# Infini-attention and GEGLU layers on one core: the first segment by halves, a plan that waits for loads, another prologue, and planner ranks that change with planned time

## The chip, the cores and the metric

The kernel runs on one core of a Trainium2 chip. The core has five engines that run side by side, each through its own list of instructions in order: TensorE (PE: matmuls, with their weight loads shown as PEld), VectorE (DVE), ScalarE (ACT), GpSimd (POOL) and SyncE (SP, which here issues the transfers). The metric is the device time of one execution in microseconds. A trace is of one profiled execution; its span runs from the first to the last instruction.

## The reference

Four steps follow each other on x of 2048 tokens by 512 features, all in bfloat16: attention, feed-forward, attention, feed-forward, each with a layer norm ahead and a residual sum behind; both attentions have the same weights, and both feed-forwards too.

```python
def _A_ref(x, wq, wk, wv, wo, beta):          # H = 32 heads of 16, N = 4 segments of L = 512
    ...
    for s in range(N):
        logits = jnp.einsum('bhqd,bhkd->bhqk', qs, ks) * scale + mask      # causal, inside the segment
        p = _softmax(logits, axis=-1)
        a_dot = jnp.einsum('bhqk,bhkd->bhqd', p, vs)
        pq = phi(qs)                                                        # t + 1 above 0, exp(t) below
        num = jnp.einsum('bhld,bhde->bhle', pq, M)
        den = jnp.einsum('bhld,bhd->bhl', pq, z)[..., None] + 1e-06
        a_mem = num / den
        o = g * a_mem + (1.0 - g) * a_dot
        outs.append(o)
        pk = phi(ks)
        M = M + jnp.einsum('bhld,bhle->bhde', pk, vs)
        z = z + jnp.einsum('bhld->bhd', pk)
    ...
def _B_ref(x, w_gate, w_up, w_down):          # hidden width 1792
    return _gelu(x @ w_gate) * (x @ w_up) @ w_down

x = x + _A_ref(_layernorm(x, axis=-1), A_wq, A_wk, A_wv, A_wo, A_beta)
x = x + _B_ref(_layernorm(x, axis=-1), B_w_gate, B_w_up, B_w_down)
x = x + _A_ref(...)
x = x + _B_ref(...)
```

A segment of an attention needs the memory M, z of the segments before it, and nothing else of them. The feed-forward works on each token by itself.

## The kernel before, in words

The work is cut into eight segments k = 0 to 7: 0 to 3 are the first attention and its feed-forward, 4 to 7 the second. Each has 512 tokens, four tiles of 128. All of x and all weights lie in SBUF. One tile `big` of PSUM holds eight banks of 512 floats.

A segment's attention: layer norm of the four tiles (statistics L544 and L553, scales on POOL L561 and L567, the normed rows L580), a transposition to `xnT` (a DMA transposition on SP, L477, or for some segments and for the feed-forward's norm in part by PE), then q, k and v by `product` (L516 to L521), which issues a matmul as four column tiles of 32. The results go from PSUM to SBUF by DVE or by ACT, whichever the plan gives them to (`evict`, L503 to L514). The scores run in steps (`steps_of`, L98): a step fills four banks with key rows times queries (L1274), one exp on ACT takes all four banks, 2048 columns, to a tile `pt` (L1344), and POOL zeroes what lies above the diagonal (L1317). A flush (L984) multiplies `pt` by the values in one bank; the values carry a column that sums the row, and DVE turns the bank (L1009), takes the reciprocal (L1013), scales (L1017) and turns back to `aT` (L1024). From the second segment on, `phi_q`, `phi_k`, `mem` and `upd` read and update the memory, and L1028 adds its part to `aT`.

The feed-forward of a segment starts with the out-projection `wo`, added to x (L1082), then a norm of its own, 14 gate tiles (gelu on ACT, from PSUM or, for the first `RAW` of them, from a copy in blocks), 14 up tiles multiplied in by DVE (L1169) and four down tiles, added to x. Segment 7, the last, is in `SPLIT`: its queries and its tokens go by halves of 256, so that the out-projection of a half needs only the four chunks of that half, and gate and up take two feature tiles of 256 columns in one bank.

The order on every engine is written out by a planner that runs while the program is built. `Clocks` and `Engine` hold a planned time for each engine; `items` are the pieces of PE work, sorted by a rank (`due`, from the tables `DUE`, `DUE_STEP` and `BIAS`, in units of a segment). The loop (L1468) takes a score step if its inputs are planned to be there and four banks are free, and else the first item in rank that is ready; if none is, it issues a filler, a product on the constant tile `warm` (L1495). Posted jobs of DVE, ACT, POOL and SP are taken by planned readiness plus a slack (`URGENT`, `PHI_SLACK` and others). PE and the other engines then run their lists in that order on the chip and wait where an input is not there.

Loads of the later x and of the weights are posted to SP with a planned time each (`X2`, `X3`, `WO`, `WG`, `WU`, `WD`, L381 to L393, L1417). The statistics of segment 2 are planned from 22.0 on (L1424) and those of segment 3 as soon as segment 1 has its keys and values (L1428); neither asks whether the rows have landed, and neither do the users of the weights.

The prologue is written by hand (L1348 to L1415): 19 warming matmuls (L417), POOL's masks and clearings (L460 to L462), the statistics of the first four tiles, scales for two tiles at a time (L1363), the first transpositions by PE (L619), and the first products of k and q; then planned time is set to 9.9 and the planner takes over.

## Time and profile before

| what | value |
|---|---|
| median of 3 runs | 563.38 us (562.55 to 564.78) |
| profiled execution | 565.31 us |
| its span | 563.6 us |
| mean granted clock of TensorE | 0.988 |
| PE busy | 543.1 us, 96% |
| DVE busy | 433.8 us, 77% |
| ACT busy | 406.1 us, 72% |
| POOL busy | 233.5 us, 41% |
| moved by DMA | 30.31 MB |

A group's row reads: line, engine, operation, output from input, shapes, count, then busy microseconds and mean nanoseconds of one, then the idle time of that engine just before these instructions and what ended it. A stretch's row reads: its start and end and length, the busy time of PE, PEld, DVE, ACT and POOL with their counts of instructions, the granted clock as a share, the busy share of the DMA engines and what they moved in GB/s. A row of the timeline reads: start, duration, engine, line, operation, output from input, shapes, count, and in brackets the idle time before and its releaser. SPq is SP's queue of transfers. Busy time of PE holds the fillers on `warm` too.

### The profile page before, as it was taken

How to read it: one execution, taken by the hardware profiler on the slowest of the kernel's cores; microseconds unless marked ns; L12 is line 12 of the kernel's file. 1: busy time of each engine (PE TensorE's matmuls, PEld its weight loads, DVE VectorE, ACT ScalarE, POOL GpSimd, SP SyncE). 2: the span in 40 equal slices, each digit the busy share in tenths (PEclk: the TensorE clock that was granted, in tenths of full speed). 3: DMA queues.
4: the chain of work that ended last, by engine and by line, in shares of the span. 5: the costliest groups of instructions: out<-in, count | busy, mean ns of one | idle time of the engine just before them, and what ended most of it. 6: DMA issues, size and time to landing. Idle time of an engine off the chain costs nothing.

```text
span 563.6 us, 28786 instructions
## 1 busy us (share of the span) xinstructions
PE 543.1 (96%) x13189; PEld 280.7 (50%) x13189; DVE 433.8 (77%) x829; ACT 406.1 (72%) x353; POOL 233.5 (41%) x403
## 2 busy tenths in 40 slices
PE   7994898999999999999999999999999999999997
PEld 3442354454454444555444444544445454555983
DVE  5985689878997887958997689979958796495361
ACT  4884789997989778938888487897879846951500
POOL 5432924554456344812467034734476333120000
PEclk9997799999999999999999999999999999999999
DMA  8298663003220102412134024241214003010001
GB/s 260 53 214 189 148 84 52 13 11 61 44 38 14 22 13 31 78 22 50 30 42 61 2 41 59 55 55 31 41 50 70 3 13 69 11 32 31 13 5 40
DMA packets 69626, 30.31 MB, mean 54 GB/s; under 512 B 54976, under 2 KB 69056, under 8 KB 69504
## 3 DMA queue, kind: packets, MB, share of 16 engines
q1 hardware_dynamic: 69360, 28.46, 26.5%
q8 instruction: 103, 1.69, 1.3%
q14 instruction: 19, 0.16, 0.1%
q10 hardware_dynamic: 144, 0.01, 0.0%
HBM read 9.71 MB, written 2.10 MB: 21 GB/s over the span
## 4 chain that ended last, share of the span: by engine, by line
PE 86%; DVE 7%; issue 2%; DMA 2%; ACT 1%; POOL 1%; SPq 1%; ACTq 0%; DVEq 0%; POOLq 0%
PE big L521 72%; PE big L1274 8%; PE big L984 6%; DVE x_sb L1082 1%; DVE st L544 1%; DMA x_sb<-in_A_x_dram 1%; ACT pt L1344 1%; DMA amT<-am 1%; DVE e L815 1%; DVE byq L1009 1%; SPq L365 1%; DVE xn L580 0%; DVE gel L512 0%; POOL vS L462 0%; POOL kB L461 0%
## 5 line engine op out<-in xcount | busy, mean ns | idle before, releaser
L1344 ACT ACTIVATE pt<-big 128x2048 bf16<-128x2048 f32 (+1 forms) x145 | 270.5, 1868 | 78.8 <-PE big L1274 72.2
L1317 POOL TENSOR_SCALAR_AFFINE_SELECT pt<-pt 64x256 bf16<-64x256 bf16 (+2 forms) x296 | 146.9, 521 | 256.7 <-ACT pt L1344 227.9
L521 PE MATMUL big<-xnT,wu_sb 128*32 128x512 bf16 (+1 forms) x2016 | 105.8, 356 | 0.9 <-DVE gel L1169 0.5
L521 PE MATMUL big<-wd_sb,gel 128*32 128x512 bf16 x1792 | 105.6, 380 | 0.4 <-DVE x_sb L1082 0.4
L521 PE MATMUL big<-xnT,wg_sb 128*32 128x512 bf16 (+1 forms) x2016 | 105.7, 356 | 0.2 <-issue 0.2
L1169 DVE TENSOR_TENSOR gel<-gel,big 128x512 bf16<-128x512 bf16 x112 | 75.1, 684 | 36.1 <-PE big L521 35.2
L521 PEld LDWEIGHTS <-wu_sb 128*32 128x32 bf16 x2016 | 52.1, 97 | 40.9 <-issue 5.6
L521 PEld LDWEIGHTS <-wg_sb 128*32 128x32 bf16 x2016 | 51.6, 97 | 40.0 <-issue 4.9
L521 PEld LDWEIGHTS <-gel 128*32 128x32 bf16 x1792 | 45.3, 97 | 43.9 <-issue 4.3
L1082 DVE TENSOR_TENSOR x_sb<-x_sb,big 128x512 bf16<-128x512 bf16 x64 | 42.8, 676 | 27.9 <-PE big L521 27.8
L1134 ACT ACTIVATE gel<-big 128x512 bf16<-128x512 f32 x70 | 38.5, 607 | 30.7 <-PE big L521 30.6
L1009 DVE STREAM_TRANSPOSE byq<-big 128x512 f32<-128x512 f32 x64 | 45.1, 704 | 16.3 <-PE big L984 9.1
L544 DVE BATCH_NORM_STATS2 st<-x_sb 128x6 f32<-128x512 bf16 x60 | 40.5, 675 | 6.4 <-DMA x_sb<-in_A_x_dram 6.1
L984 PE MATMUL big<-pt,vaug 128*32 128x192 bf16 (+4 forms) x1096 | 44.3, 266 | 0.2 <-DVE x_sb L1082 0.2
L521 PE MATMUL big<-xnT,wq_sb 128*32 128x512 bf16 (+1 forms) x528 | 36.0, 381 | 1.9 <-ACT pt L1344 1.2
L521 PE MATMUL big<-xnT,wk_sb 128*32 128x512 bf16 (+2 forms) x528 | 35.2, 380 | 0.7 <-DVE x_sb L1082 0.7
L521 PE MATMUL big<-wo_sb,aT 128*32 128x512 bf16 x512 | 32.1, 380 | 0.0
L683 POOL TENSOR_SCALAR kS<-kf,maskB 128x256 bf16<-128x256 bf16 x28 | 31.6, 1127 | 0.4
L521 PE MATMUL big<-wv_sb,xnT 128*32 128x512 bf16 x512 | 31.6, 380 | 0.0
L683 POOL TENSOR_SCALAR kS<-kf,maskA 128x256 bf16<-128x256 bf16 x28 | 29.6, 1057 | 1.6
L1274 PE MATMUL big<-q,kB 32*128 32x64 bf16 (+4 forms) x548 | 26.9, 269 | 3.3 <-ACT pt L1344 3.3
L580 DVE TENSOR_SCALAR xn<-x_sb,mv,rs 128x512 bf16<-128x512 bf16 x64 | 27.4, 477 | 3.4 <-POOL rs L567 2.7
(98 smaller groups left out, 628.0 us busy)
## 6 DMA issues: line engine op xcount, KB each, us to landing
vS<-vaug SPq DMA_DIRECT2D x16, 136.0 KB, 2.8
out_dram<-x_sb SPq DMA_DIRECT2D x16, 128.0 KB, 1.7
wg_sb<-in_B_w_gate_dram SPq DMA_DIRECT2D x8, 224.0 KB, 4.4
wd_sb<-in_B_w_down_dram SPq DMA_DIRECT2D x7, 256.0 KB, 4.7
kB<-kf SPq DMA_DIRECT2D x28, 64.0 KB, 2.9
wu_sb<-in_B_w_up_dram SPq DMA_DIRECT2D x8, 224.0 KB, 3.6
x_sb<-in_A_x_dram SPq DMA_DIRECT2D x3, 512.0 KB, 5.9
xnT<-xn SPq DMA_TRANSPOSE x48, 3.2
```

Of the source, the lines that this page charges most:

```text
L521: nc.tensor.matmul(out[r], lhsT=lhsT[:, r], rhs=rhs, start=start, stop=stop, tile_position=(0, 32 * c))
L544: nc.vector.bn_stats(out=self.st6[:, 0, :], in_=x_sb[:, self.tt0 + j, :])
L580: eng.tensor_scalar(out=xn[:], in0=x_sb[:, self.tt0 + j, :], scalar1=self.mv[:, j, 0:1], scalar2=self.rs[:, j, :], op0=ALU.subtract, op1=A ...
L683: eng.tensor_scalar(out=kS[:, b, :, :, u], in0=self.kf[:, b, :].rearrange("p (t h c) -> p t h c", h=2, c=Q)[:, :, 0, :], scalar1=(maskA, m ...
L984: nc.tensor.matmul(ps()[32 * j:32 * j + 32, q0 + shift:q1 + shift], lhsT=va[:, ki, values_of(va, b, p, j)], rhs=step["pt"][:, j, c0:c0 + q ...
L1009: nc.vector.transpose(out=self.byq[:, c], in_=ps()[:])
L1082: ck.dve.post(ck.made(), slack, (0.683, lambda: nc.vector.tensor_tensor(out=xt, in0=xt, in1=ps()[:], op=ALU.add), lambda t: (ps.read(t), t ...
L1134: return lambda: nc.scalar.activation(out=out(), in_=in_(), func=ACT.Gelu_apprx_tanh)
L1169: ck.dve.post(ck.made(), NORMAL, (0.683, lambda: nc.vector.tensor_tensor(out=hidden(g, h), in0=hidden(g, h), in1=banked(ps), op=ALU.mult), ...
L1274: nc.tensor.matmul(big[:, got[j], c0:c0 + q1 - q0], lhsT=lhsT, rhs=a.q[rows, b, q0:q1], start=True, stop=True, tile_position=(32 * j, 0))
L1317: nc.gpsimd.affine_select(out=v, in_=v, pattern=[[0, m], [by, size]], compare_op=ALU.is_ge, fill=0.0, base=by - 1, channel_multiplier=-1)
L1344: 0.172 + 0.000832 * width * len(banks_of), lambda g=g, st=st: nc.scalar.activation(out=pt[:, g, 0:width], in_=st, func=ACT.Exp, scale=SCA ...
```

## The change

- Segment 0 joins segment 7 in `SPLIT`. Its steps are new: for each block of heads the first 256 queries, then the rest. Six steps end the first half; its four chunks are flushed by halves. Out-projection, norm, gate, up and down of segment 0 go by halves of its tokens, with three of seven gate groups of a half kept raw (`RAW_FIRST`) and a rank step of their own (`HALF_DUE`).
- The plan notes when the last piece of x2, x3, wo, gate, up and down is planned to have landed (`LANDING` after its bytes). The statistics of segments 2 and 3 and, for segment 0, the out-projection, gate, up and down ask for that note. The loads have other planned times.
- The prologue: 14 warming matmuls, and none between the first transpositions and the first product; `vS` is cleared by DVE; the columns of ones in the values are written by POOL, after the first norms, and not by ACT; scales are made for one tile at a time; the second turned tile is copied by DVE; the copies stand in another order; the planner starts at 8.3.
- `Tuning`: caps on open banks, slacks and rank offsets come from a table (`TUNING`, `OFF`) and change at every 8 us of planned time (`CHANGES`, 71 entries). Constants `DUE`, `BIAS` and others have other values. `RAW` is 7 instead of 6, `GELU_TILES` 2 instead of 3.
- A flush asks for the values `vS` only if one of its pieces reads them. The planner's own loops are made shorter without another result.

```diff
-WARM = 19
+WARM = 14
+V_FIRST = -0.1396
+RAW_FIRST = 3
+HALF_DUE = 0.1367
-WO, WG, X2, WU, X3, WD = -22.6309, 21.7339, -23.7267, 48.0818, 34.2267, 25.024
+WO, WG, X2, WU, X3, WD = 16.3855, 14.7582, 5.5519, 31.0114, 59.4829, 36.5731
+LANDING = 1.5
-GELU_TILES = 3
-RAW = 6
+GELU_TILES = 2
+RAW = 7
...
+TUNING = {"CAP": 3, "CAP_FREE": 5, "AHEAD": -0.043, "EAGER": 1, "QUAD": 1, "FLUSH_WAIT": 8.768, "SOON": -0.243, ...}
+CHANGES = {
+    8.0: {"ADD": -17.428, "CAP": 5, "CAP_FREE": 5, "DIRECT": -15.134, ...},
...
+    568.0: {"FLUSH_WAIT": 9.26, "upd": 0.26, "wo": -0.274},
+}
...
-SPLIT = {NK - 1}
+SPLIT = {0, NK - 1}
...
-        found.append((shared(range(KT), (0, 1)), []))
-        found += [first(b) for b in range(KT)]
+        if k:
+            found.append((shared(range(KT), (0, 1)), []))
+            found += [first(b) for b in range(KT)]
+        else:
+            def begun(b):
+                return [(b, par, 0, 0, HALF, HALF * par) for par in range(2)]
+
+            for b in (0, 2):
+                found += [(begun(b), []),
+                          ([(c, par, 1, P, HALF, P * (2 * (c - b) + par)) for c in (b, b + 1) for par in range(2)],
+                           [(b, None, 0)]), (begun(b + 1), [(b + 1, None, 0)])]
...
+class Tuning:
+    def due(self, it):
+        return it.due + self.off[it.kind]
+
+    def turn(self, now):
+        resort = False
+        while self.changes and self.changes[0][0] <= now:
+            for name, value in self.changes.pop(0)[1].items():
+                if name in self.off:
+                    self.off[name], resort = value, True
+                else:
+                    setattr(self, name, value)
+        return resort
...
+    vS = cst.tile([P, TPS, VW + 15], BF16, name="vS")
+    nc.vector.memset(vS[:], 0.0)
-    nc.gpsimd.memset(vS[:], 0.0)
-    nc.gpsimd.tensor_scalar(out=cden[:], in0=tmp_e[:], scalar1=1.0, scalar2=None, op0=ALU.add)
-    for va in vaugs:
-        nc.scalar.activation(out=by_head(va)[:, :, :, :, DH], ...)
+    def value_columns():
+        nc.gpsimd.tensor_scalar(out=cden[:], in0=tmp_e[:], scalar1=1.0, scalar2=None, op0=ALU.add)
+        for va in vaugs:
+            nc.gpsimd.tensor_copy(out=by_head(va)[:, :, :, :, DH], ...)
...
+            def loaded(name):
+                return k > 0 or ("loaded", name) in ev
...
+    def first_norm(j):
         nc.vector.bn_stats(out=st6[j][:, 0, :], in_=x_sb[:, j, :])
         nc.vector.bn_aggr(out=n0.mv[:, j, :], in_=st6[j][:])
+        nc.gpsimd.tensor_scalar(out=v[:], in0=n0.mv[:, j:j + 1, 1:2], scalar1=EPS_LN, scalar2=None, op0=ALU.add)
+        nc.gpsimd.tensor_tensor(out=n0.rs[:, j:j + 1, :], in0=v[:], in1=mhalf[:, 0:1, :], op=ALU.pow)
...
-    ck.pe, ck.act.free, ck.dve.free, ck.pool.free, ck.sp.free = 9.9, 9.9, 12.0, 8.5, 9.0
+    ck.pe, ck.act.free, ck.dve.free, ck.pool.free, ck.sp.free = 8.3, 8.3, 11.5, 9.5, 9.0
...
+            to_come[name] -= 1
+            if not to_come[name]:
+                there = ck.dma + LANDING
+                ck.at(there, lambda: ev.update({("loaded", name): there}))
...
-    norm_of_input(2, 22.0, 1.0)
-    if N3:
-        norm_of_input(3, N3, 1.0)
-    else:
-        ck.when(lambda: ("v", 1, 3) in ev and all(("k", 1, b) in ev for b in range(4)),
-                lambda: norm_of_input(3, ck.pe, 2.0))
+    ck.when(lambda: ("loaded", "x2") in ev, lambda: norm_of_input(2, max(ck.pe, 18.0), 1.0))
+    ck.when(lambda: ("loaded", "x3") in ev and ("v", 1, 3) in ev and all(("k", 1, b) in ev for b in range(4)),
+            lambda: norm_of_input(3, ck.pe, 2.0))
```

More of the change, by code (lines that the diff above doesn't have):

```diff
@@ L181, in serve @@
     def serve(self, now):
+        if self.free > now or not self.jobs:
+            return False
         self.jobs = [j for j in self.jobs if not j[4]]
@@ L353 @@
     ck = Clocks()
+    tn = Tuning()
     ev = ck.ev
@@ L627, in insert @@
     def insert(it):
-        bisect.insort(items, it, key=lambda one: one.due)
+        bisect.insort(items, it, key=tn.due)
     e_jobs = []
@@ L1060, in flush_item @@
                               and all(c["there"].get(b, 1e9) + 0.1 <= ck.pe for c in used)
-                              and ck.has(*[("vS", k, u) for u in ((par,) if whole else range(2))])
+                              and ck.has(*[("vS", k, u) for u in ((par,) if whole else range(2)) if any(pc[1] == 2 for pc in pieces)])
                               and ck.has(*[("v", k, j) for j in rows])
@@ L1195, in down @@
                 return Item(k + DUE["down"] + BIAS.get(("down", k), 0) + DUE_STEP["down"] * j,
-                            lambda: ck.has(*[("h", k, g, h) for g in range(groups)]),
+                            lambda: ck.has(*[("h", k, g, h) for g in range(groups)]) and loaded("down"),
                             dense(ps, pairs), done, kind="down", ps=ps)
@@ L1456, in timely @@
         last = max((f for f, o in zip(banks, owner) if o == "s"), default=0.0)
-        return last <= ck.pe + AHEAD or EAGER and not opened and not any(it.ready() for it in items if it.kind != "flush")
+        return last <= ck.pe + tn.AHEAD or tn.EAGER and not opened and not any(it.ready() for it in items if it.kind != "flush")
     def score():
```

302 lines of the change are left out of this document (181 added, 121 removed).

## The prediction

> **What bounds the kernel now.** I read the page first, then the busy time by stretches of the span, then the same stretches for the filler matmuls alone, then the waits and the order of time where a stretch shows a hole.
>
> ```profile
> span 563.6 us, 28786 instructions
> ...
> PE 543.1 (96%) x13189; PEld 280.7 (50%) x13189; DVE 433.8 (77%) x829; ACT 406.1 (72%) x353; POOL 233.5 (41%) x403
> ...
> PE   7994898999999999999999999999999999999997
> ...
> PEclk9997799999999999999999999999999999999999
> ```
>
> TensorE (PE) is the bound: 96% busy. The slices show where it isn't: the fourth and fifth slice of 14.1 us, where the granted clock falls too. By stretches, with all engines:
>
> ```profile
> core 0: us, PE busy (x) PEld busy (x) DVE busy (x) ACT busy (x) POOL busy (x), PEclk, DMA share, GB/s
> ...
> 8.20:15.00 6.80, 5.80 (x122) 3.48 (x126) 4.16 (x13) 3.83 (x5) 1.58 (x2) 1.00 0.95 300
> 15.00:45.00 30.00, 30.00 (x668) 14.26 (x666) 25.21 (x57) 24.72 (x28) 10.93 (x25) 1.00 0.69 146
> 45.00:60.00 15.00, 5.24 (x92) 2.13 (x88) 9.26 (x20) 7.91 (x6) 6.21 (x9) 0.64 0.78 164
> 60.00:65.00 5.00, 5.00 (x68) 2.27 (x64) 2.12 (x3) 3.31 (x4) 4.70 (x8) 0.70 0.70 156
> ...
> 84.00:100.00 16.00, 14.56 (x396) 7.88 (x390) 15.64 (x34) 14.81 (x13) 7.07 (x13) 1.00 0.38 51
> ...
> 140.00:540.00 400.00, 397.40 (x9772) 205.23 (x9768) 315.43 (x590) 298.67 (x253) 165.96 (x282) 1.00 0.21 36
> ```
>
> From 140 to 540 us PE idles 2.60 of 400 us (0.65%): nothing is to be had there, only to be lost. Before 100 us it idles 9.76 us in the stretch 45 to 60 and 1.44 us in 84 to 100. And its busy time holds matmuls on the constant tile `warm`, which the planner puts in when it has nothing else. The same stretches for that tile:
>
> ```profile
> 15.00:45.00 30.00, 6.85 (x116) 2.92 (x120) 0.00 (x0) 1.00 0.69 146
> 45.00:60.00 15.00, 2.84 (x32) 0.80 (x24) 0.00 (x0) 0.64 0.78 164
> ...
> 65.00:84.00 19.00, 2.76 (x44) 1.07 (x44) 0.00 (x0) 1.00 0.60 104
> ...
> 100.00:140.00 40.00, 0.39 (x4) 0.11 (x4) 0.00 (x0) 1.00 0.15 28
> ```
>
> That is 12.84 us of filler after the prologue. So the loss lies wholly before 140 us. The hole itself, in order of time:
>
> ```profile
> 43.91 0.47 SPq L365 DMA_DIRECT2D x_sb<-in_A_x_dram  x1
> ...
> 49.84 0.69 DVE L544 BATCH_NORM_STATS2 st<-x_sb 128x6 f32<-128x512 bf16 x1 [6.08 <-DMA x_sb<-in_A_x_dram]
> ...
> 50.66 0.70 DVE L1009 STREAM_TRANSPOSE byq<-big 128x512 f32<-128x512 f32 x1
> ...
> 51.41 2.33 PE L521 MATMUL big<-warm 128*32 128x512 bf16 x20 [5.90 <-DVE byq L1009]
> ```
>
> The rows of x for segment 3 are issued at 43.91 and land at 49.84; VectorE (DVE) had reached their statistics 6.08 us earlier, and behind that instruction stood the transposition that frees PE's bank: PE waits 5.90 us, and its clock is down until 65 us. The clock's lowest stretch:
>
> ```profile
> 50.00:55.00 5.00, 3.30 (x60) 1.50 (x60) 4.79 (x12) 0.67 (x1) 0.00 (x0) 0.50 0.84 125
> ```
>
> **Part 1: the plan waits for loads.** Statistics of segments 2 and 3 are now planned only after their load is planned to have landed, and out-projection, gate, up and down of segment 0 wait for their weights. The wait on DVE goes: other work stands ahead of the statistics. The gain is the idle 9.76 us, and the clock: useful busy time is 5.24 - 2.84 = 2.40 us in 45 to 60, most of it at 0.50 (half, 1.2 us), and 5.00 us at 0.70 in 60 to 65 (1.5 us): 2.7 together, 12.5 in all. Late next is whatever waits for a load in the plan with too small a margin; the plan takes a load to be there 1.1 + 1.5 us and its bytes at 200 KB a us after its issue, 5.2 us for these 512 KB on an empty queue, and the row above shows 5.93. I bound a residue by nothing and by the whole 12.5 (the same stop, elsewhere) and take 2.0, nearest to the small stops of the later stretches (2.60 in 400 us), because a plan that knows the load errs by a share of a landing, not by a landing.
>
> [...]
>
> **Part 2: segment 0 by halves.** Its first query half ends after six of 19 score steps, so that the feed-forward (FFN) of its first 256 tokens can start while the second half is scored. Before, it comes very late:
>
> ```profile
> 84.00 2.12 PE L521 MATMUL big<-wo_sb,aT 128*32 128x512 bf16 x36
> ...
> 99.22 0.83 PE L521 MATMUL big<-xnT,wg_sb 128*32 128x512 bf16 x12
> ```
>
> The costliest groups of the page give the size of that work:
>
> ```profile
> L521 PE MATMUL big<-xnT,wu_sb 128*32 128x512 bf16 (+1 forms) x2016 | 105.8, 356 | 0.9 <-DVE gel L1169 0.5
> ...
> L521 PE MATMUL big<-wd_sb,gel 128*32 128x512 bf16 x1792 | 105.6, 380 | 0.4 <-DVE x_sb L1082 0.4
> L521 PE MATMUL big<-xnT,wg_sb 128*32 128x512 bf16 (+1 forms) x2016 | 105.7, 356 | 0.2 <-issue 0.2
> ...
> L1344 ACT ACTIVATE pt<-big 128x2048 bf16<-128x2048 f32 (+1 forms) x145 | 270.5, 1868 | 78.8 <-PE big L1274 72.2
> L1169 DVE TENSOR_TENSOR gel<-gel,big 128x512 bf16<-128x512 bf16 x112 | 75.1, 684 | 36.1 <-PE big L521 35.2
> ...
> L1082 DVE TENSOR_TENSOR x_sb<-x_sb,big 128x512 bf16<-128x512 bf16 x64 | 42.8, 676 | 27.9 <-PE big L521 27.8
> L544 DVE BATCH_NORM_STATS2 st<-x_sb 128x6 f32<-128x512 bf16 x60 | 40.5, 675 | 6.4 <-DMA x_sb<-in_A_x_dram 6.1
> ```
>
> Up, down and gate of one segment are an eighth of the three PE rows, 39.6 us. That work can stand where fillers stand, once it is ready. Six exps of 1.87 us from 11 us on end at 22 at the earliest. Behind the last stand eight steps of DVE (turning, reciprocal, scaling, turning back, sum, statistics, norm, eviction) of up to 0.68 us, 5 us, and PE's and POOL's between them, 4 to 6 by estimate: the first gate is possible near 32 us. So the fillers after that go (2.84 + 2.76 + 0.39 = 6.0 and none is left), and of the 6.85 in 15 to 45, which lie between 23 and 45, I let 2.8 go, since the statistics of segment 2 may be planned from 18 instead of 22 and its projections come sooner; bounds 0 and 6.85. Gain 8.8. Of the 1.44 us in 84 to 100 I take 1.0: DVE is 15.64 of 16 us busy there because out-projection, norm and memory fall together, and segment 0's share moves away.
>
> Its price on PE. Gate and up of 256 columns instead of 512:
>
> ```profile
> 514.04 6.22 PE L521 MATMUL big<-wd_sb,gel 128*32 128x512 bf16 x112
> ...
> 521.81 4.43 PE L521 MATMUL big<-xnT,wg_sb 128*32 128x256 bf16 x156
> ```
>
> 28 products of 512 take 6.22 - 0.38 = 5.84 us over 27 steps, 0.216 each; 39 of 256 take 4.43 - 0.27 = 4.16 over 38, 0.109 each. 112 products become 224: 224 x 0.109 - 112 x 0.216 = 0.2 us. Counting the lists of steps, scores go from 196 to 224 matmuls and 9,280 to 9,728 columns: 448 columns, 0.2 us at that rate, and one exp of 64 columns becomes one of 512, some 1.5 us on ACT, covered while PE has other work. The flushes keep 256 matmuls and 10,240 columns. DVE turns each chunk in two halves, four more reciprocals, scalings and turnings back, about 2 us on an engine 77% busy; without that cover it would be 2 us on PE. Two more changes between exp and gelu tables are 1.28 us each on ACT, with the same cover:
>
> ```profile
> L1134 ACT ACT_TABLE_LOAD x8 | 10.3, 1283 | 0.1
> ```
>
> I charge 1.0 us for all of it, between 0.4 and the 6.5 us without any cover, nearest to 0.4 because ACT and DVE have idle time over the span.
>
> **Part 3: the prologue.**
>
> ```profile
> 4.07 1.29 DVE L1358 BATCH_NORM_STATS2 st<-x_sb 128x6 f32<-128x512 bf16 x2 [1.33 <-DMA x_sb<-in_A_x_dram]
> ...
> 4.21 1.96 POOL L462 MEMSET vS<- 128x2236 bf16 x1
> ...
> 6.59 1.34 ACT L465 ACTIVATE vaug<-cden 128x128 bf16<-128x128 bf16 x2 [2.35 <-POOL cden L463]
> 6.63 0.23 POOL L1364 TENSOR_SCALAR ve<-mv 128x2 f32<-128x2 f32 x1
> ...
> 8.17 0.72 PE L619 MATMUL big<-ident,xn 128*128 128x128 bf16 x8 [0.91 <-DVE xn L580]
> ...
> 11.03 0.29 PE L1274 MATMUL big<-q,kf 16*128 16x256 bf16 x4 [0.49 <-DVE xnT L622]
> ```
>
> The 1.96 us clearing moves to DVE, idle until x lands at 4.07, so GpSimd (POOL) takes the first scale near 5.0 instead of 6.63, tile by tile. DVE then has the statistics of rows 2 and 3 (two of 0.68 us and their aggregation) ahead of the key copy, which gives back some: I get the first score near 9.8, a gain of 1.2 us (bounds 0 and 1.6). The 14 warming matmuls, five fewer, end before the first transposition, which DVE's norm releases in the row, and are not on the path. The value columns' two ACT copies go to POOL, about 1 us where POOL was 1.58 of 6.80 busy; if the cover is gone they delay masks by that.
>
> **Part 4: new ranks, caps and slacks, changing every 8 us of planned time.** They reorder the same instructions. In 140 to 540 the bounds are a gain of 2.6 us and a loss of 33 us at the idle rate of 84 to 100 (rival D); I take nothing beside the 2.0 us above, nearest to the 400 us row itself.
>
> **The sum.** 1.2 + 12.5 + 8.8 + 1.0 - 2.0 - 1.0 = 20.5 us. Span 563.6 - 20.5 = 543.1; the profiled execution took 565.31, so 544.8; the median of the runs, 563.38, is 1.93 lower, so 542.9, rounded to 543.
>
> **The rivals.** (B) The stop moves to the weights. Gate is now wanted near 32 us instead of 99. Out-projection's load is posted at 16.4 us of planned time instead of first of all, gate from 14.8, up from 31.0, down from 36.6, and SP issues in order, loads behind transpositions that wait for DVE:
>
> ```profile
> 21.70 6.57 SPq L477 DMA_TRANSPOSE xnT<-xn  x4
> ...
> 28.32 1.52 SPq L365 DMA_DIRECT2D wg_sb<-in_B_w_gate_dram  x3
> ```
>
> One late weight holds everything on PE, which doesn't skip. A hole of the old size: 543 + 12.5 = 555.5. For it: the loads at 28 us stood behind 6.57 us of transpositions. Against: the plan sees that queue and the landing. (C) The halves give no filling: DVE is 25.21 of 30 us busy in 15 to 45, and the FFN of segment 0 brings it 14 x 0.684 + 8 x 0.676 + 4 x 0.675 = 17.7 us and more for evictions; if DVE then sets the pace, the fillers stay: 543 + 8.8 = 551.8. Against: that is 0.45 us of DVE for each us of PE, less than the 1.1 (25.21 to 23.15 useful) of the stretch itself. (D) Slower: the new order lets DVE's queue run full in segments 1 to 7 as it does in 84 to 100, where PE idles 1.44 of 16 us, 9%. Over 400 us that is 36 - 2.6 = 33.4: 576.4. It decides from 23 of 400 us on, 5.8%. Against: the same planner's order before held 0.65% there. (E) B and C together: 543 + 21.3 = 564.3, no change.
>
> **How the numbers follow.** Forecast 0.60, own range 537 to 549 (all fillers and idle gone would be 6 us less, half of a hole, 6.2, more); B 0.13, C 0.12, D 0.11, E 0.04. To hold eight in ten the range goes from 537 up to B, 557. Faster takes forecast, B and C, 0.85; same (within 0.5%, 2.8 us, about what a measurement tells) E, 0.04; slower D, 0.11.
>
> **What would show it.** Part 1: no DVE wait on x of several us, clock 1.00 from 15 us on. Part 2: gate matmuls of 256 columns before 40 us, fillers under 5 us, none after 40. Part 3: first score before 10.2 us. Part 4: PE idle in 140 to 530 under 5 us. Wrong would make it: a PE gap over 3 us on wg, wu, wd or wo, or DVE over 90% busy past 140 us.

## The result, and the profile after

The changed kernel takes 557.66 us (median of 4 runs, 556.67 to 558.83), against 563.8 us for the kernel before (4 runs, 562.55 to 564.78): a ratio of 0.9893, 95% interval 0.9861 to 0.9925. It is faster by 6.1 us, where I had forecast 20.4 (543 us), and 0.66 us outside my range. The profiled execution took 558.45 us, with a span of 556.6 against 563.6.

First the page of the changed kernel: its span, the busy time of its engines, and of the slices those of PE and its clock.

```profile
span 556.6 us, 29574 instructions
...
PE 538.6 (97%) x13578; PEld 293.1 (53%) x13578; DVE 436.4 (78%) x836; ACT 415.4 (75%) x373; POOL 238.1 (43%) x402
...
PE   7989699999999999999999999999999999999997
...
PEclk9989999999999999999999999999999999999999
```

The fifth slice, 55.7 to 69.6 us, is still no full one. The same stretches as in the prediction, all engines, of the changed kernel:

```profile
8.20:15.00 6.80, 5.55 (x84) 3.32 (x87) 4.64 (x15) 2.26 (x2) 4.17 (x7) 0.75 1.09 355
15.00:45.00 30.00, 28.18 (x588) 13.22 (x584) 26.52 (x63) 24.93 (x24) 14.40 (x22) 0.94 0.51 118
45.00:60.00 15.00, 13.47 (x422) 9.68 (x421) 10.39 (x20) 14.13 (x15) 11.97 (x16) 1.00 1.01 199
60.00:65.00 5.00, 3.46 (x128) 2.82 (x128) 2.67 (x5) 4.15 (x5) 0.00 (x0) 1.00 1.14 251
65.00:84.00 19.00, 16.67 (x507) 11.53 (x511) 15.39 (x32) 12.48 (x10) 4.24 (x10) 1.00 0.11 20
84.00:100.00 16.00, 15.85 (x460) 8.36 (x464) 15.64 (x34) 14.63 (x13) 8.33 (x17) 1.00 0.41 68
100.00:140.00 40.00, 38.90 (x1176) 24.79 (x1169) 35.25 (x64) 35.34 (x30) 23.31 (x36) 1.00 0.22 36
140.00:540.00 400.00, 397.69 (x9968) 210.60 (x9964) 316.07 (x591) 305.24 (x273) 166.33 (x279) 1.00 0.22 38
```

The hole is gone: 45 to 60 us idles 1.53 us in place of 9.76. But 15 to 45 now idles 1.82, 60 to 65 1.54, 65 to 84 2.33 and 100 to 140 1.10 us, all stretches that were full before. From 15 to 540 us the idle time fell from 13.80 to 10.77, by 3.0 us only. And the clock is not at 1.00 from 15 us on. For the tile `warm` alone, the same kernel:

```profile
15.00:45.00 30.00, 6.48 (x92) 2.50 (x92) 0.00 (x0) 0.94 0.51 118
...
65.00:84.00 19.00, 0.82 (x12) 0.32 (x12) 0.00 (x0) 1.00 0.11 20
...
140.00:540.00 400.00, 0.40 (x4) 0.17 (x4) 0.00 (x0) 1.00 0.22 38
```

7.70 us of filler are left of 12.84; nearly all of it before 45 us, where I had let 2.8 us go and 0.37 went. The new idle time, from the order of time of PE; the bracket holds the idle time before the row and its releaser:

```profile
31.19 0.51 PE L1098 MATMUL big<-pt,vaug 128*32 128x256 bf16 x16 [1.82 <-ACT pt L1464]
...
56.31 3.35 PE L635 MATMUL big<-xnT,wg_sb 128*32 128x256 bf16 x115 [0.90 <-issue]
...
61.13 1.60 PE L635 MATMUL big<-xnT,wu_sb 128*32 128x256 bf16 x51 [1.15 <-issue]
...
67.33 0.51 PE L635 MATMUL big<-xnT,wu_sb 128*32 128x256 bf16 x11 [2.73 <-issue]
```

Three of the gaps, 4.78 us, are no wait for another engine: "issue" is time in which PE waited for nothing that the profile shows. They lie in the gate and up of segment 0, inside a product. The view of waits gives them the first place:

```profile
PE big L635 <- issue: 5.5, 5, 2.7
PE big L1098 <- ACT pt L1464: 1.8, 1, 1.8
```

The packed trace also holds transfers of the kind `instruction`, which I take for the refills of the engines' lists of instructions. Those of queue q8 are blocks of 16,384 bytes; the page's row has queue, kind, packets, megabytes and share:

```profile
q8 instruction: 106, 1.74, 1.4%
```

I take them for TensorE's, since their number follows its count of instructions: 106 for the 27,181 that this trace holds of TensorE, 256 each, 103 for 26,405 in the kernel before, and 48 for 12,475 in the run further down with every product full-width. Between 45 and 70 us of the changed kernel they are these (start and duration in us):

```
47.54 2.12
53.83 0.95
58.57 1.09
64.82 1.16
68.99 0.96
```

The refills of 53.83, 58.57 and 64.82 end at 54.78, 59.66 and 65.98, and the three gaps end 1.5, 1.5 and 1.3 us after that. Where gate and up run 256 columns wide in segment 7, with 5 GB/s of transfers from 520 to 540 us, refills start 3.3 to 4.3 us apart (520.90, 524.23, 527.70, 531.50, 535.77) and PE has one gap, of 0.34 us. That fits the size of the work: at 0.109 us a product, 3.7 us are 34 products of eight instructions each, four weight loads and four matmuls, so by this estimate 272 instructions for a block, near the 256 counted. In segment 0 the refills start 4.7 and 6.3 us apart, while the loads of up, down and x keep the DMA engines at a share of 1.10 and 1.13 (126 and 272 GB/s). So the first theory after the result was: **in segment 0's halves PE runs out of instructions, because the refill starts late behind the loads.**

Counting PE's instructions in the trace, in place of the time, supports the first half of this. The three gaps stand after its instructions 1985, 2241 and 2497, which are 256 apart: at one place of a block each time, whatever the instruction works on. At the start of the refill before each gap PE was 70, 84 and 0 instructions short of that place; at the start of all other 103 refills it was short of it by 108 or more. So these three were late. That it is the loads that make them late is not shown yet.

### The profile page after: what moved, and what is told of

The parts are those of the page before. It is cut to its first block, busy times and chain, and to the rows that moved or that the text cites. A ratio compares the mean times of both kernels' runs of the same rounds, so it can differ in the third digit from the quotient of the medians.

```text
span 556.6 us, 29574 instructions
## 1 busy us (share of the span) xinstructions
PE 538.6 (97%) x13578; PEld 293.1 (53%) x13578; DVE 436.4 (78%) x836; ACT 415.4 (75%) x373; POOL 238.1 (43%) x402
## 4 chain that ended last, share of the span: by engine, by line
PE 89%; DVE 4%; ACT 3%; issue 2%; DMA 1%; POOL 0%; SPq 0%; ACTq 0%; DVEq 0%
PE big L635 74%; PE big L1394 8%; PE big L1098 6%; ACT pt L1464 1%; ACT gel L1254 1%; DMA amT<-am 1%; DMA x_sb<-in_A_x_dram 1%; DVE x_sb L1199 0%; SPq L592 0%; DVE xn L694 0%; DVE st L1478 0%; DVE am L984 0%; POOL rs L1482 0%; ACT gel L627 0%; DVE e L929 0%
## 5 line engine op out<-in xcount | busy, mean ns | idle before, releaser
L1464 ACT ACTIVATE pt<-big 128x2048 bf16<-128x2048 f32 x145 | 272.1, 1878 | 81.6 <-PE big L1394 77.0
L1437 POOL TENSOR_SCALAR_AFFINE_SELECT pt<-pt 64x256 bf16<-64x256 bf16 (+2 forms) x288 | 150.9, 550 | 240.5 <-ACT pt L1464 237.2
L635 PE MATMUL big<-xnT,wu_sb 128*32 128x512 bf16 (+1 forms) x2240 | 107.7, 337 | 5.3 <-issue 4.6
L635 PEld LDWEIGHTS <-wu_sb 128*32 128x32 bf16 x2240 | 57.6, 97 | 41.4 <-issue 11.6
L635 PEld LDWEIGHTS <-wg_sb 128*32 128x32 bf16 x2240 | 57.9, 97 | 36.5 <-issue 6.1
L1098 PE MATMUL big<-pt,vaug 128*32 128x64 bf16 (+5 forms) x1152 | 45.1, 264 | 2.4 <-ACT pt L1464 1.8
L1254 ACT ACTIVATE gel<-big 128x512 bf16<-128x512 f32 x64 | 35.4, 604 | 8.1 <-PE big L635 8.0
L797 POOL TENSOR_SCALAR kS<-kf,maskB 128x256 bf16<-128x256 bf16 x28 | 29.5, 1054 | 0.4
L1098 PE MATMUL big<-pt,vS 128*32 128x64 bf16 x960 | 28.6, 193 | 0.7 <-issue 0.4
```

Source lines behind the costliest of these rows:

```text
L635: nc.tensor.matmul(out[r], lhsT=lhsT[:, r], rhs=rhs, start=start, stop=stop, tile_position=(0, 32 * c))
L797: eng.tensor_scalar(out=kS[:, b, :, :, u], in0=self.kf[:, b, :].rearrange("p (t h c) -> p t h c", h=2, c=Q)[:, :, 0, :], scalar1=(maskA, m ...
L1098: nc.tensor.matmul(ps()[32 * j:32 * j + 32, q0 + shift:q1 + shift], lhsT=va[:, ki, values_of(va, b, p, j)], rhs=step["pt"][:, j, c0:c0 + q ...
L1254: return lambda: nc.scalar.activation(out=out(), in_=in_(), func=ACT.Gelu_apprx_tanh)
L1437: nc.gpsimd.affine_select(out=v, in_=v, pattern=[[0, m], [by, size]], compare_op=ALU.is_ge, fill=0.0, base=by - 1, channel_multiplier=-1)
L1464: 0.172 + 0.000832 * width * len(banks_of), lambda g=g, st=st: nc.scalar.activation(out=pt[:, g, 0:width], in_=st, func=ACT.Exp, scale=SCA ...
```

## The experiments

Each ratio is against the kernel before, run on the same chip beside it.

**The wait for landed rows alone.** The kernel before, with the statistics of segment 3 planned only once x3 is planned to have landed; nothing else of the change.

```diff
+            if last:
+                there = ck.dma + 1.5
+                ck.at(there, lambda: ev.update({"x3": there}))
...
-        ck.when(lambda: ("v", 1, 3) in ev and all(("k", 1, b) in ev for b in range(4)),
+        ck.when(lambda: "x3" in ev and ("v", 1, 3) in ev and all(("k", 1, b) in ev for b in range(4)),
```

> The kernel before, with one thing of the change: the statistics of segment 3 are planned only when its load is planned to have landed. If the stop on that load was 12.5 us of loss by itself, as the prediction's first term has it (9.8 us idle, 2.7 us of clock), the time falls to about 551 and PE has no gap over 2 us. Rival: PE had no other ready work there, so that what was a stop becomes filler on the warm tile; then only the clock's part is won, some 3 us (about 561), and the filler row of 45 to 65 us grows by 5 us or more.

Measured: 565.64 us, ratio 1.0007 (0.9984 to 1.0031). Nothing is won. Stretches of all engines, and of the order of time of PE the largest gaps:

```profile
45.00:60.00 15.00, 10.59 (x236) 4.66 (x232) 10.03 (x20) 12.65 (x10) 12.09 (x19) 0.77 1.02 253
...
65.00:84.00 19.00, 15.40 (x469) 8.21 (x466) 15.40 (x33) 13.56 (x13) 6.47 (x12) 1.00 0.48 73
```

```profile
49.07 0.40 PE L1274 MATMUL big<-q,kB 32*128 32x64 bf16 x8 [1.89 <-ACT pt L1344]
...
82.68 0.40 PE L1274 MATMUL big<-q,kB 32*128 32x320 bf16 x8 [3.60 <-ACT pt L1344]
```

The single stop on DVE is gone, and behind it stand stops on the exp: PE runs through the scores, has no feed-forward to put between them, and waits for ACT. The idle time of 45 to 84 us is 8.01 where it was 9.76. Neither my theory (the hole's time is won) nor the rival (fillers grow into it) had this. The hole was a want of work, and the wait on x was only the place where it showed. The kernel before had shown part of it already: of its 9.76 us only 5.90 waited on DVE, and the rest on the exp, as these rows of its order of time have it:

```profile
56.26 0.62 PE L1274 MATMUL big<-q,kB 32*128 32x64 bf16 x8 [1.55 <-ACT pt L1344]
58.03 0.61 PE L1274 MATMUL big<-q,kB 32*128 32x320 bf16 x8 [1.15 <-ACT pt L1344]
59.80 1.90 PE L521 MATMUL big<-xnT,wq_sb 128*32 128x512 bf16 x16 [1.16 <-ACT pt L1344]
```

**The halves taken back.** The changed kernel with segment 0 whole.

```diff
-SPLIT = {0, NK - 1}
+SPLIT = {NK - 1}
```

> The changed kernel with segment 0 whole again, all else as changed. If the halves are what fills PE, fillers come back beyond 40 us, 6 us of them or more, and the time is 562 or more. Rival: what the halves win by filling they lose by doubling the matmuls of segment 0's gate and up; then the three gaps in 55 to 68 us (4.8 us) are gone and the time is 557 or less.

Measured: 588.37 us, ratio 1.0402 (1.0359 to 1.0446). After the prologue the fillers are 42.76 us, among them these, for the tile `warm` alone:

```profile
65.00:84.00 19.00, 9.06 (x140) 3.37 (x132) 0.00 (x0) 1.00 0.65 81
84.00:100.00 16.00, 6.30 (x100) 2.50 (x100) 0.00 (x0) 1.00 0.28 45
...
140.00:540.00 400.00, 15.76 (x252) 6.35 (x252) 0.00 (x0) 1.00 0.21 34
```

The gaps of "issue" are gone with the halves, but for 0.2 us. The halves are what fills PE up to 100 us. That 15.76 us appear after 140 shows that the other tables are made for this order, so the whole 31 us are not the halves' own.

**A quarter of the instructions.** Gate and up of segment 0 as one full-width matmul in place of four column tiles; order and plan as in the changed kernel.

```diff
+    def whole(out, lhsT, rhs, start=True, stop=True):
+        ck.tiling("columns")
+        nc.tensor.matmul(out, lhsT=lhsT, rhs=rhs, start=start, stop=stop)
...
-                         lambda kt=kt, f=f, n=n: product(ps()[:, n * L // self.parts:(n + 1) * L // self.parts],
+                         lambda kt=kt, f=f, n=n: (product if k else whole)(ps()[:, ...],
```

> The changed kernel with the same plan and order, but each product of segment 0's gate and up is one matmul of 128 x 128 x 256 and not four column tiles: a quarter of the instructions for the same work. Theory (the PE gaps of 0.9, 1.15 and 2.73 us in 55 to 68 us lie inside a product, so they are waits for PE's own instructions, which come by DMA behind the weight loads): the three gaps go, 4.8 us less, about 553. Rival (the weights land late): the gaps stay where they are, 557 to 558.

Measured: 552.15 us, ratio 0.9774 (0.9748 to 0.9799), 5.5 us below the changed kernel's median. All engines:

```profile
45.00:60.00 15.00, 14.48 (x260) 10.62 (x260) 10.18 (x19) 14.42 (x17) 10.08 (x12) 1.00 1.05 226
60.00:65.00 5.00, 5.00 (x90) 2.45 (x89) 4.86 (x12) 4.58 (x4) 0.00 (x0) 1.00 0.16 52
65.00:84.00 19.00, 19.00 (x518) 11.28 (x520) 17.62 (x37) 16.28 (x14) 8.01 (x16) 1.00 0.29 53
```

The stretches that idled 5.40 us together idle 0.52, under the same loads (226 GB/s). Two refills in these products now start 9.3 us apart (51.34 and 60.63), where they were 4.7 and 6.3 us apart, and no gap of "issue" is left there. The weights and the order are the same, so the rival, weights that land late, is out.

**Warming matmuls in the prologue's gaps.** Seven of them, to keep the clock up between 8 and 15 us.

```diff
+    keep_warm(1, 0)
     first_norm(2)
...
+    keep_warm(2, 1)
     ps_late, ps_high = ...
```

> The changed kernel with seven more warming matmuls, put into PE's gaps of the prologue from 6.5 to 11.3 us. Theory (those gaps, 2.1 us in five places, let the clock fall to a half from 11.6 to 15.0 us): the clock stays at 1.00 in 10 to 15 us and the time falls by 1.0 to 1.7 us, to about 556.3. Rival: the clock falls for another reason, or the seven delay the first score by as much; no gain, 557.5 or more.

Measured: 557.85 us, ratio 0.9869 (0.9844 to 0.9895). All engines:

```profile
8.20:15.00 6.80, 6.65 (x118) 3.78 (x122) 5.47 (x18) 3.35 (x4) 4.28 (x8) 1.00 1.07 358
15.00:45.00 30.00, 28.18 (x602) 13.16 (x597) 27.14 (x65) 25.16 (x24) 15.92 (x25) 0.94 0.55 127
...
60.00:65.00 5.00, 3.99 (x104) 3.23 (x106) 1.18 (x2) 1.49 (x2) 0.00 (x0) 0.66 0.57 164
```

The clock holds in the prologue, and the time doesn't move: the low clock is back later, here in 60 to 65 after a gap of "issue" of 2.79 us.

**Traffic put beside a 256-column stretch.** Eight extra stores of x of 512 KB, half of them meant for a 512-column stretch, half for segment 7's 256-column one.

```diff
+MORE = (303.0, 312.0, 524.0, 533.0)
...
+    def more():
+        for s in (1, 2):
+            rows = slice(TPS * s, TPS * s + TPS)
+            load(of[:, rows, :], x_sb[:, rows, :])
+    for at in MORE:
+        ck.at(at, more)
```

> The changed kernel with four pairs of extra 512 KB stores of x (segments 1 and 2, to their own rows of the output) that nothing waits for: two pairs at the planned times 303 and 312 us, where gate and up run 512 columns wide, two at 524 and 533 us, where segment 7's gate and up run 256 columns wide in four column tiles. Theory (TensorE's list of instructions is refilled by the same DMA engines; at 256 columns it drains about twice as fast, so a refill that stands behind bulk traffic comes too late): near 524 and 533 TensorE shows gaps of 0.9 to 2.7 us that no semaphore explains, in the middle of a product, which the changed kernel does not have there; near 303 and 312 none over 0.5 us. The time goes up by 2 to 5 us against 557.7. Rival (the gaps at 54 to 67 us belong to the weights' loads or to segment 0's place and not to bulk traffic as such): no new gap at either place, the time within 1 us.

Measured: 554.99 us in one run. By the order of SP's queue the stores ran at 309 to 317, at 512 to 517 and at 542 to 547 us: of these only one pair met 256-column products, and the stretch it met had begun at 510.5. No gap over 0.34 us came up there, as the rival said; but 4 us of traffic are about one refill, so this settles nothing. Whether it is the traffic or the place in the program that makes the refill late stays open here.

**Longer traffic at the same place.** So 5 MB instead of 1, at 524 us of planned time: the loads of the query, key and value weights, dead by then, and two stores of x, twice.

```diff
+        for n, w in (("q", A_wq), ("k", A_wk), ("v", A_wv)):
+            load(w_att[n][:], w_view(w))
+        for s in (0, 1):
+            load(of[:, rows, :], x_sb[:, rows, :])
```

> The changed kernel with 5 MB of traffic that nothing waits for while segment 7's gate and up run 256 columns wide in four column tiles: the query, key and value weights loaded again into their own place and the first two segments' rows of x stored again, all of it twice. In the run with extra stores the only 1 MB that fell into this stretch (512 to 516.5 us) made no gap; here the traffic lasts about 15 us, as it does in segment 0. Theory (TensorE's list of instructions drains every 3.7 us at 256 columns, and its refills start late while many transfers are queued, whatever these carry): between 512 and 530 us refills lie over 4.5 us apart, and one to three gaps of 0.9 to 2.8 us in the middle of a product come up, where the changed kernel has none over 0.34. Rival (it is the place, the first refills after the attention of segment 0, or the weights' own arrival): refills stay at 3.6 to 4.0 us, no gap over 0.5 us.

Measured: 557.06 us in one run. First all engines in 505 to 530 us of the changed kernel:

```profile
505.00:530.00 25.00, 25.00 (x817) 20.62 (x813) 9.82 (x19) 11.22 (x18) 0.93 (x2) 1.00 0.07 20
```

and the same stretch with the traffic, and PE's order of time in it:

```profile
505.00:530.00 25.00, 22.12 (x676) 18.37 (x672) 7.12 (x13) 10.13 (x16) 0.93 (x2) 0.93 0.69 224
```

```profile
521.49 5.78 PE L636 MATMUL big<-xnT,wg_sb 128*32 128x256 bf16 x144 [2.88 <-issue]
```

TensorE's refills start at 512.34 and then at 519.23 only, 6.9 us apart, and the gap of 2.88 us ends 1.38 us after the second one's end at 520.11. Nothing waited for these transfers. The gap stands after PE's instruction 25,537, at the same place of a block as those of segment 0. That is the theory's sign at a place where the changed kernel has none: beside 325 GB/s from 512 to 524 us, where the changed kernel has 17, a refill started late, and PE, at four column tiles of 256 columns, stood still from 518.61 to 521.49. The traffic didn't delay each one: the next refill, at 524.12, came in time, though the traffic went on until about 527 us. What decides which refill is late no run here shows. After 530 us the refills lie 3.4 to 3.8 us apart again.

**Segment 2's norm later.** It competes for DVE with segment 1's: from 20 to 31 us DVE of the changed kernel is busy 10.69 of 11.00 us.

```diff
-    ck.when(lambda: ("loaded", "x2") in ev, lambda: norm_of_input(2, max(ck.pe, 18.0), 1.0))
+    ck.when(lambda: ("loaded", "x2") in ev, lambda: norm_of_input(2, max(ck.pe, 30.0), 1.0))
```

> The changed kernel with segment 2's norm from 30 us of planned time instead of 18. Theory (between 20 and 30 us VectorE is full, and segment 2's statistics and normalization stand ahead of segment 1's, so that TensorE fills with warming matmuls): fillers in 15 to 45 us fall from 6.5 us to under 4, the last transposition of segment 1's input comes before 29 us, and the time falls by 2 to 3 us to about 555. Rival (segment 1's own chain of norm, queries, keys and features sets it, or the fillers only move to where segment 2 is wanted): fillers from 15 to 84 us in all within 1 us of the 7.3 of the changed kernel, the time 557 to 560.

Measured: 573.16 us, ratio 1.0142 (1.0117 to 1.0168). The fillers in 15 to 45 us do fall, as the theory said, but the time rises by 15.5 us, which neither said. The fillers there, and the waits of PE:

```profile
15.00:45.00 30.00, 3.80 (x64) 1.62 (x64) 0.00 (x0) 0.94 0.55 154
```

```profile
PE big L1394 <- ACT pt L1464: 6.1, 8, 1.7
```

Stops on the exp of 6.1 us come up, and 3.7 more in the flushes: work that stood between the score steps now comes later. From 140 to 540 us, far from the moved norm, PE idles 11.00 us in place of 2.31, so much of the loss is the tables' fit to the old order; what the later norm costs by itself the run doesn't tell.

**The table of changes left empty.** `CHANGES = {}`; the base ranks and slacks hold throughout.

> The changed kernel with the table that alters ranks and slacks as planned time goes on left empty: the base values hold throughout, and the plan is made anew. Theory (the table tunes the order after 140 us, where TensorE is busy 99.4%, and is there to make up for what the halves upset): slower by 5 to 25 us, 563 to 583, with idle and filler time that returns between 45 and 540 us. Rival (the table is worth nothing measurable and the order that the base values give is as good): within 3 us of 557.7.

Measured: 576.56 us, ratio 1.0209 (1.0174 to 1.0243). The waits of PE:

```profile
PE big L1322 <- ACT pt L1392: 16.4, 29, 1.6
```

29 stops on the exp, 16.4 us. From 140 to 540 us PE idles 12.33 us, where the changed kernel idles 2.31. The theory holds: with these base values the table is what keeps the rest of the span full. Whether other base values could do without it is not tested.

**Both ends full-width.** Segment 7's gate and up too.

```diff
-                         lambda kt=kt, f=f, n=n: (product if k else whole)(
+                         lambda kt=kt, f=f, n=n: (whole if self.parts == 2 else product)(
```

> The run with segment 0's gate and up as full-width matmuls (552.15 us), and segment 7's, the other one in halves, full-width as well. Theory (a refill is late only behind bulk traffic, and there is none while segment 7 runs): no gain beyond the first, 552.2 within 1 us, and the stretch from 500 us on takes as long as in that run. Rival (a 256-column matmul in four column tiles costs TensorE more by itself, by its issue): segment 7's 128 products of gate and up are shorter by 10 ns each at least, 1.3 us or more off, under 551.

Measured: 549.70 us (549.12 to 551.26), ratio 0.9722 (0.9693 to 0.9751): the best of all. It is 2.45 us below the run with one end, but those stood beside medians of before of 565.43 and 564.92, and the intervals overlap, so the second end isn't shown to matter. In the two profiles the stretch from segment 7's first 256-column gate matmul to the end takes 41.42 us in place of 41.88, some 0.5 us less. The group of gate products of this kernel, and then of the changed one:

```profile
L640 PE MATMUL big<-xnT,wg_sb 128*128 128x256 bf16 x224 | 26.0, 273 | 0.0
```

```profile
L635 PE MATMUL big<-xnT,wg_sb 128*32 128x256 bf16 x896 | 26.4, 273 | 0.9 <-issue 0.9
```

Over 224 products, those of both ends, full width is 0.4 us shorter in all, so the rival's 10 ns each is not there; what goes is the idle time.

**All gate and up, and every product, full-width.** First the one, then the other, each against the changed kernel.

```diff
-                         lambda kt=kt, f=f, n=n: product(ps()[:, n * L // self.parts:(n + 1) * L // self.parts],
+                         lambda kt=kt, f=f, n=n: whole(ps()[:, ...],
```

```diff
-        for c in range(4):
-            r = slice(32 * c, 32 * c + 32)
-            nc.tensor.matmul(out[r], lhsT=lhsT[:, r], rhs=rhs, start=start, stop=stop, tile_position=(0, 32 * c))
+        nc.tensor.matmul(out, lhsT=lhsT, rhs=rhs, start=start, stop=stop)
```

> Gate and up of all eight segments as full-width matmuls, in place of four column tiles each; order, plan and arithmetic as in the changed kernel. Theory (the column tiles cost time only where the list of instructions runs dry, and at 512 columns it does not): the same as with both ends full-width, 549.7 within 1.5 us. Rival (four column tiles hide the loading of weights that a full-width matmul shows): slower, 168 products of two layers' segments in the middle show up to 20 ns each, up to 13 us over the six segments, 555 to 563.

> Every product that the changed kernel does in four column tiles (transpositions by TensorE, queries, keys, values, memory, output projection, gate, up, down) as one full-width matmul, 12452 rows on TensorE in place of 27158; order and plan as in the changed kernel. Theory (refills are rare and no longer late anywhere): at most 1 us better than with both ends alone, 548 to 550. Rival (changing between the four row tiles of the scores, the column tiles of the flushes and full width costs TensorE a drain at each change): slower, up to 0.1 us at each of some hundred changes, 555 to 570.

Measured: 558.87 us, ratio 0.9894 (0.9849 to 0.9939), for gate and up of all segments, and 556.72 us, ratio 0.9852 (0.983 to 0.9874), for every product. Both lose most of what both ends won. The page's busy times with both ends and with every product:

```profile
PE 535.4 (97%) x12234; PEld 287.2 (52%) x12234; DVE 435.5 (79%) x836; ACT 415.1 (76%) x373; POOL 233.9 (43%) x402
```

```profile
PE 541.9 (98%) x6225; PEld 263.5 (48%) x6225; DVE 437.5 (79%) x836; ACT 415.6 (75%) x373; POOL 236.7 (43%) x402
```

PE is busy 6.5 us longer, though the groups of gate, up and down are not longer than with both ends. So the loss lies where products meet other forms. The traces show at which: I took the time from the start of the last matmul of one form to the start of the first of the next, leaving out what is over 0.8 us, which I take for waits. From a product to a flush, which stays in column tiles, it is 0.20 us on average with both ends and 0.31 with every product full-width (49 changes each); from a flush to a product 0.07 and 0.16 us (51 and 50 changes). That is 9.7 us more, and all the rest of PE's time gives 3.8 back. To the scores and from them nothing is added (0.30 and 0.21 us in both runs). So the rival was right that a change between full width and column tiles costs some 0.1 us, but not for the row tiles of the scores. With gate and up alone full-width, their changes to flushes and to the other products, 85 in all, take 7.1 us more than with both ends. The waits view shows the same at the weight loads of the flushes, first with both ends, then with every product:

```profile
PEld L1103 <- issue: 3.8, 14, 0.7
```

```profile
PEld L1096 <- issue: 19.4, 52, 0.6
```

Why such a change costs this, no run here shows.

**The changed kernel again,** for a second profile.

> The changed kernel once more, unaltered, for a second profile. Theory: the gaps in the middle of gate and up between 54 and 68 us are the kernel's own and come back, two to four of them with 4 to 6 us in all; the half clock at 11.6 to 15.0 us comes back too, since TensorE's gaps of the prologue set it. Rival: the gaps or the half-clock stretch are an accident of one execution and move or vanish, with the time of that execution 2 to 5 us shorter.

Measured: 562.41 us in one run. PE's order of time shows the gaps of the first profile, and one more wait:

```profile
35.46 1.06 PE L635 MATMUL big<-xnT,wq_sb 128*32 128x512 bf16 x16 [2.86 <-DMA xnT<-xn]
...
60.59 3.35 PE L635 MATMUL big<-xnT,wg_sb 128*32 128x256 bf16 x115 [1.94 <-issue]
...
67.06 2.96 PE L635 MATMUL big<-xnT,wu_sb 128*32 128x256 bf16 x51 [2.79 <-issue]
```

They come back before the same groups of 115 and 51 matmuls, with 1.94 and 2.79 us, and end 1.31 and 1.35 us after the ends of the refills started at 58.20 and 64.56; a third of 1.23 stands in the scores at 54.67. All three stand at the same place of a block, after PE's instructions 1729, 1985 and 2241, the one in the scores too. The half clock of 11.6 to 15.0 us does not come back; it stands at 36.4 to 39.8 and 67.1 to 70.5 us instead. So the gaps are the kernel's own, their size is 0.90 to 2.79 us in the two profiles, and the low clock in the prologue is not fixed to the kernel.

## Why the prediction was wrong, by its own steps

The sum was 20.5 us of span; 7.0 came. By the rows above:

| term | predicted | measured |
|---|---|---|
| idle of PE after 15 us (9.76 + 1.0 - 2.0) | 8.8 | 3.0 |
| clock after the hole, and elsewhere | 2.7 | -0.8 |
| fillers after 15 us | 8.8 | 5.1 |
| prologue less the price of the halves (1.2 - 1.0) | 0.2 | -0.3, the remainder |
| sum | 20.5 | 7.0 |

The measured clock is the 2.7 us of before, less 1.7 us (a quarter of 6.80) and 1.8 us (0.06 of 30) in the changed kernel.

**Where the stops go (the residue of 2.0 us) is the step that failed most.** I took 2.0 us because a plan that knows the loads errs by little. The plan's times for the loads were not the matter: no gap of PE over 1 us from 15 us to 540 us waits on a weight or on x in the first profile. 5.0 us were to be left after 15 us and 10.77 were, among them the three gaps of 4.78 us and a stop of 1.82 us on the exp at 31.19. What failed is a resource I had not looked for. Rival B put a stop among the weights of segment 0 and named SP's queue; the stop came in the same products, but on a refill of TensorE's own list of instructions, which started late beside the loads. In the price of the halves I had counted 224 products against 112 at 0.216 and 0.109 us, and found 0.2 us; I had not counted that the eight instructions of a product are then used up in 0.109 us in place of 0.216. A row of my own prediction, segment 7's gate at 256 columns, could not show it: from 514 to 526 us the DMA engines of the kernel before moved 36 GB/s, and PE was busy all 12.00 us. Full-width products take it back: 5.5 us. The signs I had set for being wrong, a gap over 3 us on a weight or DVE over 90% busy, did not come, since neither looks at this list.

**Part 1's 12.5 us was given to the wrong part.** The wait on x goes, but alone it wins nothing (565.64 us beside 565.43); the idle time moves to the exp, where 3.86 of the 9.76 us had stood before. It is the halves that fill it.

**The fillers were over-sized in time.** My chain put the first gate of segment 0 near 32 us. In the changed kernel the out-projection of the first half stands at 37.98 and the first gate at 51.73 us. So the fillers of 24 to 34 us had nothing to take their place (6.48 of 6.85 left); those after 45 us went, all but 0.82 and 0.40 of 6.0. DVE is what is full there: from 20 to 31 us it is busy 10.69 of 11.00 us, with segment 1's and 2's norms and the first half's chunks in one queue. Rival C named this engine and these fillers. Its ratio of DVE time to PE time was an average and said nothing of the order in which DVE takes the work. Taking segment 2's norm out of it lowers the fillers and costs more elsewhere.

**The prologue's 1.2 us was right in its place and too small.** The first score moves from 11.03 to 9.28 us, 1.75 us and more than my upper bound of 1.6, as this row of the changed kernel shows:

```profile
9.28 0.29 PE L1394 MATMUL big<-q,kf 16*128 16x256 bf16 x4 [0.48 <-ACT q L1501]
```

In the profiled execution the half clock from 11.6 to 15.0 us takes 1.7 us of it back by my estimate, a quarter of 6.80. I had dropped the five warming matmuls at no cost. Putting seven in holds the clock (1.00 from 8.2 to 15 us) and wins nothing, and in the second profile it holds without them (1.00 too), so they are not shown to be the cause.

**The clock.** I gave 2.7 us back and charged nothing for gaps to come. The low stretches of the first profile are 11.6 to 15.0 and 32.1 to 35.5 us, 3.4 us long each. By my estimate each cost 1.7 us, half its length: sixteen matmuls of 512 columns took 1.96 us at 13.18 and 1.05 us at 15.81, after the clock had come back. The two profiles of this one kernel show 0.75 and 1.00 in 8.2 to 15 us. The switches of the first profile lie on one grid of 3.41 us (11.59, 15.00, 32.07, 35.48); the gap of 1.82 us before 31.19 lies inside one stretch of this grid, and the clock is halved from 32.07 on, while the gap of 2.73 us before 67.33 lies across two, 1.6 and 1.1 us, and the clock stays. The refill gaps of 2.79 us in the second profile and 2.88 us beside the long traffic lie inside one, and 3.4 us of half clock follow each. Whether the place on the grid decides it these few gaps don't show.

**Part 4, and the rest of the span, held.** Nothing gained, nothing lost: 2.31 of 400 us idle in place of 2.60, and DVE at 79% there. Rival D did not come. With the table left empty idle time does return there (12.33 us), but the stops are on the exp and not, as the rival had it, on DVE.

With both ends full-width the span is 549.5, still 6.4 above my 543.1: idle time of 6.72 after 15 us where I had 5.0, 6.72 of fillers where I had 4.0, and 2.0 that I can't place.

## What to carry to other kernels

In this kernel products in four column tiles of 256 columns had a block of 256 instructions refilled every 3.3 to 4.3 us (segment 7), and beside the loads of segment 0 PE stood still there for 4.78 us in three gaps. So count instructions per microsecond, and where that is highest, try to keep sustained transfers away or to issue full-width matmuls there, and only there: here each change between full width and column tiles cost some 0.1 us. A gap in the middle of a product that no semaphore explains, beside a busy DMA row (a share of 1.10 and 1.13 here), is the sign to look for. And when a wait is removed, ask first which work will stand in its place: here, with the wait on x gone and nothing in its place, the idle time of 45 to 84 us went from 9.76 only to 8.01 us and moved to the exp.

## What was not expected of the hardware

What follows is from the traces of these runs. In the first profile of the changed kernel the `instruction` transfers of queue q8, which I take for TensorE's refills, are blocks of 16,384 bytes. In segment 7, at four column tiles of 256 columns and with 5 GB/s of transfers (520 to 540 us), they start 3.3 to 4.3 us apart, and PE has one gap, of 0.34 us. In segment 0, beside 221, 126 and 272 GB/s, three of them start 6.3, 4.7 and 6.3 us after the one before, and PE stood still there for 0.90, 1.15 and 2.73 us; in the run with long traffic, beside 325 GB/s (512 to 524 us), one starts 6.9 us after the one before, and PE stood still for 2.88 us. At the start of the three late refills of the first profile PE was 70, 84 and 0 instructions short of the place where it stood still, at all others 108 or more. All 13 gaps of this kind of 0.8 us or more, in the two profiles of the changed kernel and in the runs with warming matmuls, with extra stores, with long traffic and with segment 2's norm later, are 0.8 to 2.9 us long, end 1.2 to 1.5 us after the end of a refill and stand at the same place of a block of 256 instructions. The refills that ended these gaps took 0.9 to 1.6 us, and all 106 of the first profile 0.88 to 2.12 us: what is late is their start.

Every product full-width, in place of both ends alone, cost PE 6.5 us of busy time (541.9 against 535.4 us) with about half the matmuls (6,225 in place of 12,234): some 0.1 us at each change between products and flushes. Full-width gate and up won 5.5 us at the first end (552.15 against 557.66 us) and 8.0 us at both (549.70 us).
